# Two attention and gated-MLP layers on one core: new planner settings, a planned pause of GpSimd, and a last gate in two steps

## The chip, the core and the metric

The kernel runs on one core of a Trainium2 chip. A core has five engines that run side by side, each with its own instruction stream: TensorE (PE, matmuls; its weight loads are shown as PEld), VectorE (DVE), ScalarE (ACT), GpSimd (POOL) and SyncE (SP), which here issues the DMA transfers. They wait for each other on semaphores. Matmuls write to PSUM, which here is used as eight banks of 128 partitions by 512 fp32 values; the other tensors lie in SBUF. The metric is the device time of one execution in microseconds, lower being better, given as the median of several runs.

## The reference

A residual stream of 2048 tokens by 512 features passes through attention, a gated MLP, attention and a gated MLP; both attentions use the same weights, and so do both MLPs.

```python
x = x + attn(layernorm(x)); x = x + mlp(layernorm(x))      # and both once more

def attn(x):                       # 32 heads of 16, one shared key and value head
    q = (x @ wq) as 32 heads;  k = x @ wk;  v = x @ wv     # k, v: 2048 x 16
    p = softmax(q @ k.T / 4)                               # 32 x 2048 x 2048
    return heads(p @ v) @ wo

def mlp(x):                        # two halves of 896
    z = gelu(x @ w_in);  z1 = z[:, :896];  z2 = layernorm(z[:, 896:])
    g = w_sp @ z2 + b_sp[:, None]                          # mixes the 2048 tokens
    return (z1 * g) @ w_out
```

Inputs and output are bfloat16.

## The kernel before, in words

Nothing in the kernel's text fixes the order of instructions. The Python program builds a list of tasks with their dependencies, and a planner (`Sched`, and the `step_` functions of `Kernel`) walks through a model of time: whenever an engine is free in the model, its step function picks a task, and the pick is appended to that engine's stream. Only the order and the semaphore waits that the data need are emitted. A moment in which the planner left an engine idle on purpose is not in the program: on the chip an engine starts its next instruction as soon as its data and buffers are there. Every constant of the class (`SHARE`, `PV_EFF` and so on) is a setting of this planner.

**Attention.** The scores of one layer are 2048 blocks of 128 keys by 512 query columns. A score block is one matmul with a contraction of 32 rows, so four of them fit side by side in the array as row tiles; they are issued in packs of up to four (`issue_pack`, matmul at line 1227), each block to one PSUM bank. A block then goes one of two ways:

- to ScalarE (`pick_exp`, `do_exp`, line 1402), which takes exp of one block (128x512) or of two in adjacent banks (128x1024) and writes bfloat16 to slots of `Pb`, a pool of 32 slots of 128x512;
- to VectorE (`dve_block`), which approximates exp by three ramps in 16-bit integers whose bits are read as bfloat16. The first ramp reads PSUM (line 1316, task "A") and frees the bank. The second and third read the first ramp's slot (line 1335, tasks "S") and may run on GpSimd or on VectorE; two ramps whose sources lie in adjacent slots are joined into one instruction of 128x1024 (`commit_ramp`).

`SHARE`, `SHARE_HI` and `RAMP_SHARE` give the part of the blocks that goes to VectorE; the last is used while a layer's first two groups of query columns wait for their key tiles (`A.full` is not yet set).

P.V (`do_pv`, line 1457) multiplies each finished slot by V. Its output has 32 rows, so four matmuls run side by side as column tiles; a round is one matmul for each of up to four columns. `pv_depth` decides whether a round may start with fewer than four (`PV_EFF`, `PV_LEAST`) and how many rounds one task takes (`PV_MAX`). A change between score tiles, P.V tiles and full-size matmuls is a change of the array's shape, and the planner adds a cost for it in `commit`. When TensorE has been little used, `keep_warm` (line 1574) issues matmuls with zero weights.

**The rest.** Query columns are finished in eight chunks. After each, the sum is normalised, projected by `wo`, added to the residual `X` and normalised again (VectorE statistics, `L602`, `L603`; scaling on GpSimd or VectorE). Groups of chunks then enter the MLP: matmuls at lines 976 and 1022, gelu on ScalarE between two table loads. The token mixing (`spatial`) is done in five passes over source tiles; partial sums are kept in `gp` in fp16 (VectorE, line 1091). The last pass (`last_pass`) takes the last source tile: an identity matmul brings `gp` into PSUM (line 1114), the last product is added to it there (line 1116), VectorE multiplies by `z1` (line 1124), and the output projection (line 1138) and residual add (line 1142) follow. In layer 1 this overlaps with the opening of layer 2, in which each finished tile of `X` is normalised, transposed by DMA and turned into keys and values (lines 731 and 734); in layer 2 it is the tail of the kernel. SP's stream holds the loads, the transposing DMAs of tiles and of the mixing weights, and the 16 stores.

Of the kernel before, what the change touches and what calls it, by code (L numbers as in the profile page):

```python
# [92 lines left out]
class Sched:  # L93
# [69 lines left out]
    def commit(self, task, eng=None):  # L163
        t = self.t
        eng = eng or task.eng
        task.eng = eng
        if task.alts is not None:
            task.cost, task.fn = task.alts[eng]
        task.start = t
        if task.hook is not None:  # L170
            task.hook(task)
        cost = task.cost() if callable(task.cost) else task.cost
        occ, lat = cost
        if eng == "pe" and task.mode != self.pe_mode:
            occ += 100
            self.pe_mode = task.mode
        port = eng == "dve" and task.tag in PORT
        if port:
            occ += max(0.0, self.free["pool"] - t)
        end = t + occ  # L180
        self.free[eng] = end
        if port:
            self.free["pool"] = max(self.free["pool"], end)
        self.busy[eng] += occ
        task.done = end + lat
        waits = self._waits(eng, task)
        if eng == "sp":
            k = min(range(self.NDMA), key=lambda i: (self.dma_last[i].done if self.dma_last[i] else -1.0))
            prev = self.dma_last[k]
            if prev is not None:  # L190
                waits += self._wait_on(eng, prev)
            self.dma_n[k] += 16
            task.key, task.val = ("dma", k), self.dma_n[k]
            self.dma_last[k] = task
        else:
            self.cnt[eng] += 1
            task.key, task.val = eng, self.cnt[eng]
        s = dict(self.know[eng])
        if s.get(task.key, 0) < task.val:
            s[task.key] = task.val  # L200
        self.snap[(task.key, task.val)] = s
        self.prog[eng].append((waits, task.fn, task.key, task))
        self.log.append((eng, t, end, task.tag))
        if eng == "pe":
            self.pe_log.append((t, end))
        self.left -= 1
        for s_ in task.succ:
            s_.nopen -= 1
            if s_.nopen == 0:
                self._arm(s_)  # L210
        self.event(end)
        self.event(task.done)
        while self.after:
            self.after.pop(0)()
        return task
# [164 lines left out]
class Kernel:  # L380
# [4 lines left out]
    PV_FREE = 6  # L385
    KT_ACT = 16
    CREDIT = 2
    CAP_LINE = 8000
    RAMP_SHARE = 0.3
# [7 lines left out]
    SHARE = 0.3  # L397
    SHARE_HI = 0.32
# [3 lines left out]
    ACT_LOW = 1200  # L402
    POOL_MAX = 1400
    DVE_MAX = 1500
    DVE_HIGH = 2500
    PV_MIN = 3
    PV_MAX = 3
    PV_EFF = 0.7
    PV_LEAST = 4
    SLACK = 300  # L410
    SLACK_HI = 500
    MISC_T = 2000
    MISC_T2 = 1500
    MISC_T3 = 1000
    PE_LINE2 = 8000
    ACT_ONE = 3
# [688 lines left out]
    def last_pass(self, B, t, s0, n, sl, lds, zd, final, use):  # L1105

        tc, o = t // 4, (t % 4) * P
        hs = []
        for f0, f1 in ((0, 4), (4, NF)):
            def gf(e, b, lo, hi, f0=f0):  # L1110
                ins = None
                for f in range(lo, hi):
                    out = self.ps32[:, b, (f - f0) * P:(f - f0 + 1) * P]
                    e.matmul(out, self.ident16[:], self.gp[:, tc, f, o:o + P], start=True, stop=False)
                    for i in range(n):
                        ins = e.matmul(out, self.z2[:, (s0 + i) % 8, f * P:(f + 1) * P],
                                       self.wstr[:, sl[i // 4][1] + i % 4, o:o + P], start=False, stop=(i == n - 1))
                return ins
            m = f0 + 2

            def mk(lp, bank, f0=f0, f1=f1):
                def fn(e):
                    z = self.z1[:, tc, f0:f1, o:o + P]
                    return e.tensor_tensor(z, self.ps32[:, bank(), 0:(f1 - f0) * P].rearrange("p (f c) -> p f c", f=f1 - f0), z, ALU.mult)  # L1124
                return Task("dve", c_ps((f1 - f0) * P), fn, [lp] + B.z1g[tc], 0.9 + 0.08 * t, tag="gate")
            deps = [self.t_ident16] + [B.gpw[(tc, f)] for f in range(f0, f1)] + lds + zd
            made, outs = self.job(2 + 0.08 * t, [(lambda e, b, gf=gf, f0=f0, m=m: gf(e, b, f0, m), c_mm(2 * (n + 1), 128), deps),
                                                 (lambda e, b, gf=gf, m=m, f1=f1: gf(e, b, m, f1), c_mm((f1 - m) * (n + 1), 128), [])],
                                  [mk], "SPD", kind=B.layer, spare=1)
            hs += outs  # L1130
            use += made
            B.all += made
            self.gp_last.append(made[-1])
# [19 lines left out]
    def pack_ready(self):  # L1153
# [5 lines left out]
        if room < self.FILL_MIN or room < 4 and self.act_backlog() > self.ACT_LOW:  # L1159
# [9 lines left out]
        if not blks or len(blks) < room and len(blks) < 4 and A.nxt + len(blks) < len(A.blocks) and self.act_backlog() > self.ACT_LOW:  # L1169
# [20 lines left out]
    def issue_pack(self, A, blks, deps, bs):  # L1190
# [3 lines left out]
        x = self.RAMP_SHARE if not A.full else self.SHARE if self.pe_line() > self.PE_LINE else self.SHARE_HI  # L1194
# [11 lines left out]
        best = None  # L1206
        for act in itertools.combinations(sorted(bs, key=lambda b: b.i), len(aj)):
            runs = sum(1 for x, y in zip(act, act[1:]) if y.i != x.i + 1)
            key = (runs, sum(b.i for b in act))
# [44 lines left out]
    def slot_runs(self):  # L1254
        free = {b.i: b for b in self.pslots.avail()}
# [12 lines left out]
    def first_slot(self):  # L1268

        runs = self.slot_runs()  # L1270
        free = {b.i: b for r in runs for b in r}
# [22 lines left out]
    def dve_block(self, pk, u, kt, j, bank, n):  # L1294
# [10 lines left out]
        def h0(task):  # L1305
            b, paired = self.first_slot()
            slot(0, b, task, T)
            if not paired:
                self.open_slots.append(b.i)

            def go():
# [3 lines left out]
        lo0 = float(TERMS[0][0])  # L1315
        a = self.dve(c_ps(512), lambda e: e.tensor_scalar(self.Pi[:, sl[0].i, :], self.ps32[:, bank.i, :], EBIAS + lo0, lo0, op0=ALU.add,  # L1316
                                                          op1=ALU.max), [pk], 1.0, gate=lambda: self.slot_ok(n, 1), hook=h0, tag="A")
# [14 lines left out]

    def ramp_fn(self, v, src, dst, k):
        lo = float(TERMS[v][0])
        return lambda e: e.tensor_scalar(self.Pi[:, dst():dst() + k, :], self.Pi[:, src():src() + k, :], lo, 1.0, op0=ALU.add, op1=ALU.mult)  # L1335

    def commit_ramp(self, k, eng):

        s = self.s
        v, sl, n = k.ramp  # L1340
        for it in s.arm[eng]:
            p = it[2]
            if p.ramp is None or p.start is not None or p.ready > s.t or p.ramp[0] != v or abs(p.ramp[1][0].i - sl[0].i) != 1:
                continue
            m = max(n, p.ramp[2])
# [5 lines left out]
            two = sorted((k, p), key=lambda x: x.ramp[1][0].i)  # L1351
            i, o = two[0].ramp[1][0].i, run[0].i
            f = Task(eng, (c_pool if eng == "pool" else c_4x)(1024), self.ramp_fn(v, lambda: i, lambda: o, 2), k.deps + p.deps, tag="S")
# [7 lines left out]
            for x in two:  # L1361
                x.start, x.done, x.key, x.val = f.start, f.done, f.key, f.val
                s.left -= 1
            return
        s.commit(k, eng)

    def pick_exp(self):
        q = [x for x in self.act_q if x[0].done <= self.s.t][:self.ACT_MAX]
        av = sorted((b for b in self.pslots.items if not b.held and b.free <= self.s.t), key=lambda b: b.i)
# [149 lines left out]
    def pv_depth(self, pv, room):  # L1519
# [5 lines left out]
        if hurry:  # L1525
            most = max(most, 1)
        for r in range(most, 0, -1):
# [120 lines left out]
    def step_dve(self):  # L1648
        s = self.s
        k = s.pick("dve", lambda k: k.alts is None or "pool" not in k.alts)  # L1650
# [10 lines left out]

    def step_pool(self):
        k = self.s.pick("pool")
# [130 lines left out]
```

## Time and profile before

| | |
|---|---|
| median of 3 runs | 1654.17 us (1652.5 to 1657.26) |
| profiled execution | 1656.29 us |
| its span, first to last instruction | 1654.6 us |
| mean granted TensorE clock | 0.988 |
| exp on ScalarE (L1402) | 946 of 128x512, 948 of 128x1024 |
| first ramps on VectorE (L1316) | 1254 |
| second and third ramps (L1335) | GpSimd 976 of 128x512, 421 of 128x1024; VectorE 218 and 236 |
| score and P.V matmuls | 4096 and 6604 |

The span is what the trace covers. Busy time is the union of an engine's instructions; an instruction's own duration can overlap its neighbour's in the engine's pipeline, so durations can add up to more than the busy time. TensorE's ends are modelled, and a busy TensorE need not be at its peak. A row of the groups gives line, engine, operation, output and inputs with shapes, count, busy time, mean duration of one, and then the idle time of the engine just before such instructions with what ended it. A row of the waits gives who waited for whom, the total in us, the number of times and the longest.

### The profile page before, as it was taken

The numbers are of one execution on the slowest core, as the hardware profiler recorded it, in microseconds if no ns is written. First come the engines' busy times: TensorE is split into PE (matmuls) and PEld (weight loads), VectorE is DVE, ScalarE is ACT, GpSimd is POOL, SyncE is SP. The second block draws the span as 40 slices with busy tenths as digits, with TensorE's granted clock in tenths as the row PEclk, the third lists the DMA queues.
The fourth block names the chain that finished last, engine by engine and source line by source line (L and its number), as shares of the span: only waits on it lengthen the run. The fifth ranks groups of instructions, "written<-read, shape, count | busy, mean of one in ns | idle before, by whom it ended". The sixth has DMA issues, their size and how long they took to land.

```text
span 1654.6 us, 36692 instructions
## 1 busy us (share of the span) xinstructions
PE 1539.3 (93%) x13877; PEld 528.1 (32%) x14016; DVE 1405.0 (85%) x2556; ACT 1447.2 (87%) x2067; POOL 1182.1 (71%) x1616
## 2 busy tenths in 40 slices
PE   6999999999999999999988998999999999899998
PEld 3333233222322223233433332322223222222345
DVE  7899878898788887987978998788887998888877
ACT  5999999999899999995447999999998999899940
POOL 6878868778678767874456877777876778778730
PEclk8999999999999999999999999999999999999999
DMA  8000000100000110101110000011000101101021
GB/s 208 14 8 5 8 8 17 33 17 17 11 20 21 21 21 14 27 17 36 24 30 17 9 4 8 7 30 33 14 14 14 27 14 27 13 14 27 17 40 54
DMA packets 123996, 39.76 MB, mean 24 GB/s; under 512 B 116272, under 2 KB 123312, under 8 KB 123824
## 3 DMA queue, kind: packets, MB, share of 16 engines
q1 hardware_dynamic: 123824, 37.41, 10.7%
q8 instruction: 115, 1.88, 0.5%
q14 instruction: 57, 0.47, 0.1%
HBM read 6.98 MB, written 2.10 MB: 5 GB/s over the span
## 4 chain that ended last, share of the span: by engine, by line
PE 51%; ACT 30%; DVE 13%; issue 3%; POOL 2%; DMA 1%; SPq 0%; DVEq 0%; ACTq 0%; POOLq 0%
ACT Pb L1402 30%; PE ps_all L1457 16%; PE ps_all L1227 14%; PE ps_all L1083 7%; DVE Pb L1316 5%; PE ps_all L976 3%; PE ps_all L1022 3%; DVE Pb L1335 2%; PE ps_all L1138 2%; POOL Pb L1335 1%; PE ps_all L761 1%; DVE gp L1091 1%; PE ps_all L920 1%; PE ps_all L834 1%; DVE ln_st L602 1%
## 5 line engine op out<-in xcount | busy, mean ns | idle before, releaser
L1402 ACT ACTIVATE Pb<-ps_all 128x512 bf16<-128x512 f32 (+1 forms) x1894 | 1351.2, 884 | 78.7 <-PE ps_all L1227 66.9
L1335 POOL TENSOR_SCALAR Pb<-Pb 128x512 int16<-128x512 int16 (+1 forms) x1397 | 1064.1, 762 | 306.9 <-DVE Pb L1316 134.7
L1316 DVE TENSOR_SCALAR Pb<-ps_all 128x512 int16<-128x512 f32 x1254 | 830.0, 684 | 139.1 <-PE ps_all L1227 124.1
L1457 PE MATMUL ps_all<-Pb,V 128*32 128x512 bf16 x6604 | 628.4, 390 | 15.3 <-ACT Pb L1402 5.9
L1227 PE MATMUL ps_all<-Q,kT 32*128 32x512 bf16 x4096 | 572.6, 387 | 49.5 <-ACT Pb L1402 28.7
L1227 PEld LDWEIGHTS ps_all<-Q,kT 32*128 32x128 bf16 x4096 | 146.8, 91 | 543.6 <-ACT Pb L1402 309.6
L1457 PEld LDWEIGHTS ps_all<-Pb,V 128*32 128x32 bf16 x6604 | 150.2, 94 | 307.8 <-issue 125.9
L1335 DVE TENSOR_SCALAR Pb<-Pb 128x1024 int16<-128x1024 int16 (+1 forms) x454 | 205.0, 474 | 17.4 <-PE ps_all L1457 14.0
L1083 PE MATMUL ps_all<-wstr,z 128*128 128x512 bf16 x744 | 193.9, 380 | 18.0 <-issue 7.5
L1091 DVE TENSOR_TENSOR gp<-ps_all,gp 128x512 f16<-128x512 f32 x168 | 113.0, 687 | 26.4 <-PE ps_all L1083 24.6
L1083 PEld LDWEIGHTS ps_all<-wstr,z 128*128 128x128 bf16 x840 | 67.4, 98 | 102.7 <-issue 15.4
L1138 PE MATMUL ps_all<-w_out,z 128*128 128x512 bf16 x212 | 53.5, 380 | 3.1 <-DVE z L1124 0.8
L976 PE MATMUL ps_all<-w_in,xnT 128*128 128x448 bf16 x256 | 52.2, 360 | 2.6 <-DMA xnT<-xn 2.4
L1036 ACT ACTIVATE z<-ps_all 128x512 bf16<-128x512 f32 (+1 forms) x60 | 31.3, 566 | 23.6 <-PE ps_all L1022 23.6
L593 POOL TENSOR_SCALAR ln_rs<-ln_mv 128x1 f32<-128x1 f32 (+2 forms) x48 | 11.2, 237 | 56.3 <-DVE ln_mv L603 54.8
L1022 PE MATMUL ps_all<-xnT,w_in 128*128 128x512 bf16 (+2 forms) x274 | 50.2, 336 | 0.3
L818 DVE CAST oT<-ps_all 128x512 bf16<-128x512 f32 x64 | 43.7, 683 | 5.7 <-PE ps_all L1457 5.3
L989 DVE BATCH_NORM_STATS2 st<-z 128x6 f32<-128x448 bf16 x64 | 36.4, 607 | 12.3 <-ACT z L981 12.1
L1091 DVE TENSOR_TENSOR gp<-ps_all,bspc 128x512 f16<-128x512 f32 x56 | 38.4, 686 | 9.1 <-PE ps_all L1083 8.1
L602 DVE BATCH_NORM_STATS2 ln_st<-X 128x6 f32<-128x512 bf16 x64 | 43.2, 680 | 3.2 <-DMA X<-in_A_x_dram 3.0
L593 POOL TENSOR_SCALAR rs<-mv 128x4 f32<-128x4 f32 (+2 forms) x10 | 2.3, 234 | 55.9 <-DVE mv L991 55.9
L761 PE MATMUL ps_all<-z,wq 128*128 128x128 bf16 x512 | 40.7, 224 | 0.3 <-DVE Pb L1316 0.2
(67 smaller groups left out, 697.2 us busy)
## 6 DMA issues: line engine op xcount, KB each, us to landing
out_dram<-X SPq DMA_DIRECT2D x16, 128.0 KB, 1.7
w_in<-in_B_w_in_dram SPq DMA_DIRECT2D x1, 1792.0 KB, 12.0
X<-in_A_x_dram SPq DMA_DIRECT2D x3, 512.0 KB, 7.1
bspc<-in_B_b_sp_dram SPq DMA_DIRECT2D x8, 128.0 KB, 3.5
w_out<-in_B_w_out_dram SPq DMA_DIRECT2D x1, 896.0 KB, 12.7
wstr<-in_B_w_sp_dram SPq DMA_TRANSPOSE x40, 4.2
X<-in_A_x_dram SPq DMA_DIRECT2D x2, 256.0 KB, 3.6
wq<-in_A_wq_dram SPq DMA_DIRECT2D x1, 512.0 KB, 5.2
```

Source lines behind the costliest of these rows:

```text
L602: a = self.dve(c_ps(512), lambda e, t=t: e.bn_stats(st[:, t, :], X[:, t, :]), [dep], prio, tag="lnst")
L761: ins = e.matmul(self.ps32[:, b, g * P:(g + 1) * P], self.wq[:, kd, g * P:(g + 1) * P], self.xnT(t, kd), start=(kd == 0), stop=(kd == KD - 1))
L976: ins = e.matmul(self.ps32[:, b, 0:448], self.xnT2[:, buf, kd, o:o + P], self.w_in[:, kd, FH + h * 448:FH + (h + 1) * 448], start=(kd == 0 ...
L1022: ins = e.matmul(self.ps32[:, b, i * nq:(i + 1) * nq], self.w_in[:, kd, f * P:(f + 1) * P], self.xnT2[:, buf, kd, 0:nq], start=(kd == 0), ...
L1083: ins = e.matmul(self.ps32[:, b, :], self.z2[:, (s0 + i) % 8, f * P:(f + 1) * P], self.wstr[:, sl[i // 4][1] + i % 4, :], start=(i == 0), ...
L1091: return Task("dve", c_ps(512), lambda e: e.tensor_tensor(self.gp[:, tc, f, :], self.ps32[:, bank(), :], src, ALU.add), dps, 1.05, tag="gp")
L1138: ins = e.matmul(self.ps32[:, b, :], self.z1[:, tc, f, o:o + P], self.w_out[:, f, :], start=(f == 0), stop=(f == NF - 1))
L1227: ins = e.matmul(self.ps32[:, jb[i].i, :], self.kT[32 * j:32 * j + 32, u.half, kt * P:(kt + 1) * P], q, tile_position=(32 * j, 0), start=T ...
L1316: a = self.dve(c_ps(512), lambda e: e.tensor_scalar(self.Pi[:, sl[0].i, :], self.ps32[:, bank.i, :], EBIAS + lo0, lo0, op0=ALU.add, op1=AL ...
L1335: return lambda e: e.tensor_scalar(self.Pi[:, dst():dst() + k, :], self.Pi[:, src():src() + k, :], lo, 1.0, op0=ALU.add, op1=ALU.mult)
L1402: return e.activation(self.Pb[:, s0:s0 + n, :], self.ps32[:, b0:b0 + n, :], ACTF.Exp, scale=ESCALE)
L1457: ins = e.matmul(self.ps32[32 * j:32 * j + 32, u.bank.i, :], self.V[:, var, kt, :], self.Pb[:, sl.i, :], tile_position=(0, 32 * j), start= ...
```

## The change

The change has four parts.

1. *Settings.* More blocks for VectorE in the full part of a layer (`SHARE` 0.30 to 0.32, `SHARE_HI` 0.32 to 0.34), none in the opening of layer 2 (`RAMP_SHARE1` 0), where score packs are issued only four at a time (`FILL_R` 4, `ACT_LOW_R` 0). P.V rounds are planned only when full (`PV_EFF` 0.7 to 0.97), a change to P.V's shape needs six or more matmuls (`PV_LEAST`), one task takes at most two rounds. `ACT_ONE` 3 to 9 lets ScalarE join two blocks more often or less, by what is queued; `DVE_HIGH` and the `MISC_T` settings move too, and the planner's cost for a change of shape goes from 100 to 110 ns.
2. *Slots kept for pairs.* Where a first ramp has taken a slot, a free neighbour is kept (`kept`) for the next one, so that the later ramps of both can be joined, as long as eight other slots are free. Banks for blocks of VectorE are chosen adjacent where possible.
3. *Pairs on VectorE, and the pause.* When GpSimd's planned backlog is over 4000 ns and GpSimd is free in the plan, VectorE first looks for two joinable ramps (`ramp_pair`). When VectorE will be free within 200 ns, GpSimd takes nothing in the plan (`HOLD`).
4. *The last gate of layer 2* (`NOID`). The identity matmuls are left out; VectorE adds the PSUM product to `gp` in place, and GpSimd multiplies `z1` by `gp`. Layer 1 is left as it was.

```diff
-            occ += 100
+            occ += 110
-    PV_FREE = 6
+    PV_FREE = 8
+    KEEP = 8
+    POOL_TOP = 4000
+    HOLD = 200
+    A_ADJ = 1
-    SHARE = 0.3
-    SHARE_HI = 0.32
+    SHARE = 0.32
+    SHARE_HI = 0.34
+    FILL_R = 4
+    NOID = (False, True)
+    ACT_LOW_R = 0
+    RAMP_SHARE1 = 0.0
-    DVE_HIGH = 2500
+    DVE_HIGH = 1800
-    PV_MAX = 3
-    PV_EFF = 0.7
-    PV_LEAST = 4
+    PV_MAX = 2
+    PV_EFF = 0.97
+    PV_LEAST = 6
-    ACT_ONE = 3
+    ACT_ONE = 9
...
     def last_pass(self, B, t, s0, n, sl, lds, zd, final, use):
-                    e.matmul(out, self.ident16[:], self.gp[:, tc, f, o:o + P], start=True, stop=False)
+                    if not noid:
+                        e.matmul(out, self.ident16[:], self.gp[:, tc, f, o:o + P], start=True, stop=False)
...
+            if noid:
+                def pf(e, f0=f0, f1=f1):
+                    z = self.z1[:, tc, f0:f1, o:o + P]
+                    return e.tensor_tensor(z, self.gp[:, tc, f0:f1, o:o + P], z, ALU.mult)
+                outs = [self.pool((240 + self.PTT * (f1 - f0) * P, 60), pf, outs + B.z1g[tc], 0.9 + 0.08 * t, tag="gatep")]
...
+    def kept(self):
+        free = {b.i for b in self.pslots.avail()}
+        r = set()
+        for i in self.open_slots:
+            for k in (i + 1, i - 1):
+                if k in free and k not in r:
+                    r.add(k)
+                    break
+        return r if len(free) - len(r) >= self.KEEP else set()
...
     def step_dve(self):
+        if s.free["pool"] <= s.t + self.PORT_WAIT and self.backlog("pool") > self.POOL_TOP:
+            k = self.ramp_pair("dve")
+        if k is None:
+            k = s.pick("dve", lambda k: k.alts is None or "pool" not in k.alts)
...
     def step_pool(self):
-        k = self.s.pick("pool")
+        if s.t < s.free["dve"] <= s.t + self.HOLD and self.backlog("pool") > self.POOL_TOP:
+            return False
```

## The prediction

> **What bounds the kernel now.** I read the busy totals first, then the busy time by stage, then the waits of ScalarE, then one microsecond-scale stretch of TensorE, then the prices by shape. The totals:
>
> ```profile
> PE 1539.3 (93%) x13877; PEld 528.1 (32%) x14016; DVE 1405.0 (85%) x2556; ACT 1447.2 (87%) x2067; POOL 1182.1 (71%) x1616
> ```
>
> Four engines are nearly full, so the average decides nothing. I cut the span at ScalarE's table loads, which separate ten stages of exp from the gelu batches, and asked for busy time in each. Columns: window, length, then PE, PEld, DVE, ACT, POOL busy (instructions), clock, DMA share, GB/s.
>
> ```profile
> 0.00:229.40 229.40, 204.40 (x2073) 72.87 (x2077) 196.02 (x385) 206.68 (x300) 177.94 (x256) 0.97 0.19 45
> 241.50:419.40 177.90, 166.55 (x1520) 49.51 (x1529) 158.15 (x278) 175.30 (x237) 141.66 (x190) 1.00 0.11 22
> 785.70:1048.30 262.60, 240.68 (x2395) 92.75 (x2407) 229.42 (x436) 205.34 (x299) 180.13 (x254) 1.00 0.08 16
> 1448.60:1563.20 114.60, 109.64 (x988) 33.98 (x996) 101.25 (x175) 112.73 (x159) 92.04 (x121) 1.00 0.10 21
> 1607.70:1654.60 46.90, 42.49 (x357) 25.68 (x361) 34.43 (x59) 1.45 (x2) 0.30 (x1) 1.00 0.17 54
> ```
>
> ScalarE idles 2.6 us of 177.9 and 1.9 of 114.6; over the eight exp stages other than the first of each layer it idles 20 of 977 us. There ScalarE sets the time. Not in the stage that opens layer 2 (57.3 idle of 262.6) and in the tail, where it has no work. Its waits agree:
>
> ```profile
> ACT Pb L1402 <- PE ps_all L1227: 66.9, 73, 10.9
> ACT Pb L1402 <- PE ps_all L1457: 7.1, 13, 1.4
> ```
>
> The first (waiting for scores) lies mostly in the layer openings: 40.0 us of it between 786 and 880. The second is ScalarE waiting until a P.V round frees a Pb slot; it is small now. TensorE:
>
> ```profile
> 314.24 0.40 PE L1457 MATMUL ps_all<-Pb,V 128*32 128x512 bf16 x4
> 314.57 0.39 PE L1227 MATMUL ps_all<-Q,kT 32*128 32x512 bf16 x3
> 314.90 0.83 PE L1457 MATMUL ps_all<-Pb,V 128*32 128x512 bf16 x10
> 315.66 0.39 PE L1227 MATMUL ps_all<-Q,kT 32*128 32x512 bf16 x3
> ```
>
> From start to start, one round takes 0.33 us and three rounds (x10) 0.76: 0.215 us a round, however many of its four column tiles are used, and 0.11 us for each change between score, P.V and full shape.
>
> Prices (busy, mean ns of one):
>
> ```profile
> L1402 ACT ACTIVATE Pb<-ps_all 128x1024 bf16<-128x1024 f32 x948 | 953.2, 1098 | 51.7 <-PE ps_all L1227 45.7 <-PE ps_all L1457 3.8 <-DVE Pb L1335 0.6
> L1316 DVE TENSOR_SCALAR Pb<-ps_all 128x512 int16<-128x512 f32 x1254 | 830.0, 684 | 139.1 <-PE ps_all L1227 124.1 <-PE ps_all L1457 4.0
> L1335 POOL TENSOR_SCALAR Pb<-Pb 128x512 int16<-128x512 int16 x976 | 615.1, 630 | 225.8 <-DVE Pb L1316 111.5 <-PE ps_all L1457 40.5 <-DVE Pb L1335 10.0
> L1335 POOL TENSOR_SCALAR Pb<-Pb 128x1024 int16<-128x1024 int16 x421 | 448.9, 1066 | 81.1 <-DVE Pb L1316 23.3 <-PE ps_all L1457 23.0 <-DVE Pb L1335 7.8
> L1335 DVE TENSOR_SCALAR Pb<-Pb 128x1024 int16<-128x1024 int16 x236 | 130.9, 570 | 9.1 <-PE ps_all L1457 6.3 <-POOL Pb L1335 0.4
> L1335 DVE TENSOR_SCALAR Pb<-Pb 128x512 int16<-128x512 int16 x218 | 76.8, 370 | 8.3 <-PE ps_all L1457 7.7
> ```
>
> Exps overlap their neighbours, so these means are too high for a sum: in the instruction records, start to start without idle, a 512 exp takes 0.486 us on average and a 1024 one 0.916.
>
> **What the Trainium skill says.** "Perfetto Trace Analysis", Identifying the Most-Contended Engine: matmul busy time is a poor measure of TensorE. It agrees: 1,985 P.V and some 1,355 score rounds at 0.215, 2,679 changes at 0.11 and some 430 us of full-shape matmuls make 1,440 us, not 1,539. "TensorEngine Tiling (Array Packing)", Key Properties: changing the tiling mode drains TensorE; the 0.11 us above is that. "GPSIMD Engine Reference", Specifications: GpSimd's SBUF interfaces are shared with VectorE, which contends when VectorE runs in a two-port mode. The records show it: of 236 paired ramps on VectorE 93 began with GpSimd idle and took 0.364 us, 143 began inside a GpSimd operation and took 0.615 (up to 1.25; the wait ends with that operation). Singles: 0.209 against 0.441.
>
> **The change, part by part**, from the order in which both programs stand.
>
> *ScalarE.* 512 exps 946 to 956, 1024 exps 948 to 923: 10 x 0.486 - 25 x 0.916 = -18.1 us. By stage it is more useful: first stage of layer 1 (163 and 132 become 173 and 121) -5.2; the other four of layer 1 -11.0; first stage of layer 2 (167 and 126 become 128 and 156) +8.5, since its opening gives VectorE no block any more; the other four of layer 2 -10.4. Where ScalarE is full these are the path: -5.2 - 11.0 - 10.4 = -26.6. The +8.5 falls where it idles.
>
> *Opening of layer 2.* From the first residual add at 792 to the last key tile at 885 the pace is VectorE's and TensorE's (8.5 to 9.5 us busy in each 10). Ahead of the last key tile stand 92 score blocks instead of 120, 88 P.V matmuls instead of 182 and 54 shape changes instead of 112. TensorE saves 58 x 0.11 + about 28 rounds of P.V and 9 of scores x 0.215 = 14 us; VectorE about 36 first ramps x 0.605 (start to start) = 22. Both cover the same time: I take 18. ScalarE does 92 x 0.47 = 43 us there instead of about 84 x 0.47 = 39. Its idle time falls by 18 + 4 = 22, the stage by 22 - 8.5 = 13.5. On SP's queue one weight slab moves ahead of ten of the opening's tile transposes; it waits for layer 1's last gate to free its buffer, and keys behind it wait too. So the ends are 0 (the opening hangs on that, or on LayerNorm chains) and 22. The other slabs move by a transpose or three, among transfers that no engine waits long for.
>
> *TensorE elsewhere.* P.V rounds 1,985 to 1,737 (full ones 1,117 to 1,623), changes 2,679 to 2,265, identity matmuls 224 to 112, 120 more warming matmuls (30 rounds): -248 x 0.215 - 414 x 0.11 - 112 x 0.055 + 6 = -99 us. Outside the opening and the tail it is hidden behind ScalarE; I count nothing. It buys banks sooner for ScalarE, which has only 20 us left to regain.
>
> *VectorE.* First ramps +40 x 0.662 (830.0/1254) = +26; paired ramps +135 x 0.555 = +75; single ones -107 x 0.352 = -38: +64 us. It is hidden by 181 us of VectorE idle in the ten exp stages; with stages 40 us shorter about 77 remain. That thin a cover leaks: a late VectorE frees score banks late. I allow 10.5 us, about 1% of the saturated stretches, between 0 and 30. The pause is in the planner only: nothing holds GpSimd on the chip, so a pair may meet an operation just begun.
>
> *GpSimd.* -393 x 0.630 + 155 x 1.066 = -82 us; it idles already.
>
> *Last gate, layer 2, all in the tail.* TensorE loses 112 identity matmuls at 0.055: -6.2. VectorE's 32 adds cost what its multiplies did (0.679 and 0.547). New: 32 GpSimd multiplies with two inputs, which no row shows. Lower end, GpSimd's one-input price: 0.63 and about 0.5, 1.1 us a tile, hidden behind TensorE's 1.9 (7 x 0.055 + 7 x 0.215). Upper end, an estimate from "GPSIMD Engine Reference", Elementwise, side-by-side cycle accounting (2.6 cycles an element at 1.2 GHz) with 0.19 us of start: 1.30 + 1.02 = 2.3 us a tile, 37 for 16, and the tail is then GpSimd's: first gate at 1613, products to about 1651, then the last projection, add and store, as now. The tail gains 6 or nothing: -2. The 16 stores keep their place behind the adds.
>
> **Sum.** -26.6 - 13.5 - 2 + 10.5 = -31.6, against the profiled execution (1656.3, span 1654.6, 1.7 around it): 1624.7. It stands 2.1 above the median of the runs, so 1622 as a median.
>
> **Rivals.**
> 1. *The port takes it.* If every ramp on VectorE meets a busy GpSimd, ramps cost 371 x 0.615 + 111 x 0.441 = 277 us against 186 now; with +26 that is 118 more on 1,288 busy in 1,469 us of exp stages. At the most that VectorE can be full, say 96.5%, they need 1,457: 12 saved, with the tail 14: 1640. For it: GpSimd was busy at 143 of 236. Against: GpSimd has 82 us less to do.
> 2. *More than the sum:* pairs find GpSimd idle (0.364), VectorE's load falls, no allowance, opening -22, tail -6: -55, 1600.
> 3. *Slower: slots.* Full rounds hold Pb slots longer, and slots are kept for pairs. 365 exps now wait for a P.V matmul in the program, 306 before. Today 13 such waits cost 7.1 us, 0.55 each. The 42 us of gain before the allowance are gone when 77 of the 365 cost that; at 102 the time is 1668. Against: the share of exps that wait so hardly rises.
> 4. *Nothing:* a gain in ScalarE work that comes back as idle of equal size: 1654.
>
> **How the numbers follow.** Sum as worked 0.50 (own range 1608 to 1635), rival 1 0.17, rival 2 0.18, rival 3 0.10, rival 4 0.05. A measurement tells about 0.3%, 5 us. Faster 0.85, same 0.05, slower 0.10. The range 1597 to 1650 leaves out the low end of rival 2, rival 3 and most of rival 4.
>
> **What would show it.** Right: exp groups near 956 and 923 with ScalarE idle still under 5 us in the middle stages; about 250 us for the opening stage of layer 2; ScalarE's wait for P.V under 20 us; VectorE about 1,470 busy. Wrong: pairs near 0.8 us and VectorE at 97% of a stage; ScalarE waiting 50 us on P.V; a GpSimd multiply over 1.4 us with TensorE idle in the tail.

## The result and the profile after

The changed kernel takes 1643.24 us (median of 4 runs, 1641.84 to 1645.47), the kernel before 1655.72 beside it (4 runs, 1652.5 to 1657.65). The ratio is 0.9928 with a 95% interval of 0.9906 to 0.9949: 12 us faster. Forecast were 1622 and a range of 1597 to 1650. The direction and the range held; of the gain of 32 us only 12 came.

The totals of the changed kernel, from its page:

```profile
PE 1480.0 (90%) x13974; PEld 498.6 (30%) x14104; DVE 1452.0 (89%) x2624; ACT 1441.8 (88%) x2052; POOL 1139.3 (69%) x1410
```

TensorE has become lighter by 59 us of busy time and GpSimd by 43; VectorE is busy for 47 us more. The span fell from 1654.6 to 1640.1, and ScalarE is busy for 5 us less, not for 18. The busy time in the stages between ScalarE's table loads, for the same five stages as before (window, length, PE, PEld, DVE, ACT, POOL, clock, DMA share, GB/s):

```profile
0.00:229.60 229.60, 194.85 (x2092) 68.41 (x2096) 208.59 (x405) 204.06 (x299) 166.42 (x237) 0.98 0.21 45
243.00:417.60 174.60, 161.66 (x1526) 46.79 (x1532) 164.69 (x293) 170.04 (x241) 134.87 (x159) 0.98 0.11 22
788.90:1037.50 248.60, 218.77 (x2370) 86.36 (x2380) 208.94 (x402) 214.24 (x289) 128.48 (x172) 0.99 0.08 15
1434.20:1554.10 119.90, 110.41 (x1046) 33.84 (x1055) 113.85 (x198) 114.88 (x155) 94.03 (x112) 1.00 0.12 20
1598.90:1640.10 41.20, 36.22 (x241) 18.44 (x243) 32.52 (x57) 1.52 (x3) 32.20 (x33) 1.00 0.20 61
```

The gain is in the third row, the stage that opens layer 2 (262.6 to 248.6), and in the last, the tail (46.9 to 41.2). In the second row ScalarE now idles 4.6 us and VectorE 9.9; before it was 2.6 and 19.8. Summed over the eight exp stages other than the first of each layer (the middle stages from here on), VectorE went from 88.3% to 93.4% busy and ScalarE's idle time from 20.0 to 39.5 us. The waits, ScalarE's first, then TensorE's waits for VectorE to free a bank before scores:

```profile
ACT Pb L1460 <- PE ps_all L1252: 61.8, 120, 5.8
ACT Pb L1460 <- PE ps_all L1515: 7.9, 23, 0.8
PEld ps_all L1252 <- DVE Pb L1374: 135.9, 298, 1.4
PE ps_all L1252 <- DVE Pb L1374: 33.1, 87, 1.1
```

ScalarE waits for a score pack 120 times instead of 73. The wait for P.V (second line) stayed small. The last two lines, score packs waiting for VectorE, were in the kernel before:

```profile
PEld ps_all L1227 <- DVE Pb L1316: 84.1, 204, 1.1
PE ps_all L1227 <- DVE Pb L1316: 6.9, 19, 0.8
```

One stretch of TensorE in the changed kernel:

```profile
300.48 0.39 PE L1252 MATMUL ps_all<-Q,kT 32*128 32x512 bf16 x3
300.80 0.62 PE L1515 MATMUL ps_all<-Pb,V 128*32 128x512 bf16 x8
301.35 0.39 PE L1252 MATMUL ps_all<-Q,kT 32*128 32x512 bf16 x3
```

Two full rounds (x8) take 0.55 us start to start with their change of shape, as 2 x 0.215 + 0.11 says. The prices by shape (busy, mean ns of one):

```profile
L1460 ACT ACTIVATE Pb<-ps_all 128x1024 bf16<-128x1024 f32 x923 | 923.8, 1069 | 54.6 <-PE ps_all L1252 44.3 <-PE ps_all L1515 4.3 <-DVE Pb L1379 1.2
L1374 DVE TENSOR_SCALAR Pb<-ps_all 128x512 int16<-128x512 f32 x1294 | 842.6, 680 | 86.7 <-PE ps_all L1252 78.5 <-PE ps_all L1515 1.5
L1379 POOL TENSOR_SCALAR Pb<-Pb 128x512 int16<-128x512 int16 x583 | 371.4, 637 | 185.0 <-DVE Pb L1374 91.8 <-PE ps_all L1515 52.3 <-DVE Pb L1379 4.1
L1379 POOL TENSOR_SCALAR Pb<-Pb 128x1024 int16<-128x1024 int16 x576 | 615.8, 1069 | 155.0 <-DVE Pb L1374 86.4 <-PE ps_all L1515 26.2 <-DVE Pb L1379 8.4
L1379 DVE TENSOR_SCALAR Pb<-Pb 128x1024 int16<-128x1024 int16 x371 | 222.1, 618 | 5.9 <-PE ps_all L1515 4.6
L1379 DVE TENSOR_SCALAR Pb<-Pb 128x512 int16<-128x512 int16 x111 | 40.9, 375 | 3.3 <-PE ps_all L1515 3.3
```

A paired ramp on VectorE became dearer, 618 ns on average instead of 570. The instruction records say why. Of 371 pairs 161 began with GpSimd idle and took 0.347 us; 210 began inside a GpSimd operation and took 0.704 us. Of those 210, 119 met an operation that had started less than 0.3 us earlier; before it was 48 of 143. Not every pair that began inside an operation waited for it: 43 of the 210 ended before it, after 0.33 us, and 167 ended after it (17 and 126 before). The plan has no such meetings. In `commit`, in both kernels, GpSimd counts as busy until a second or third ramp of VectorE has ended, and in the changed kernel it also idles for the last 200 ns before VectorE comes free, so that VectorE's pair goes first. Nothing in the program of either kernel makes GpSimd wait for the pair. In the stretch below it waits only for the first ramp that VectorE has just finished (the brackets give its idle time and what ended it), so the same moment frees VectorE for two pairs and releases GpSimd, which starts before the second of them. The timeline of VectorE, then of GpSimd:

```profile
556.22 1.60 DVE L1379 TENSOR_SCALAR Pb<-Pb 128x1024 int16<-128x1024 int16 x2
557.74 1.27 DVE L1374 TENSOR_SCALAR Pb<-ps_all 128x512 int16<-128x512 f32 x2
558.94 1.59 DVE L1379 TENSOR_SCALAR Pb<-Pb 128x1024 int16<-128x1024 int16 x2
```

```profile
556.39 1.15 POOL L1379 TENSOR_SCALAR Pb<-Pb 128x1024 int16<-128x1024 int16 x1 [1.72 <-DVE Pb L1374]
559.10 1.15 POOL L1379 TENSOR_SCALAR Pb<-Pb 128x1024 int16<-128x1024 int16 x1 [1.55 <-DVE Pb L1374]
```

Twice GpSimd, idle for over 1.5 us, starts 0.16 to 0.17 us after the first of two pairs on VectorE has begun, and 0.25 us before that pair ends. In the records VectorE comes free at 556.64; the second pair, then inside GpSimd's operation, ends at 557.82. Two pairs take 1.6 us instead of the 0.75 that they need alone (e_wait, below).

### The profile page after: what moved, and what is told of

Same layout as the page of the kernel before. It is cut to its first block, busy times and chain, and to the rows that moved or that the text cites. A ratio compares the mean times of both kernels' runs of the same rounds, so it can differ in the third digit from the quotient of the medians.

```text
span 1640.1 us, 36572 instructions
## 1 busy us (share of the span) xinstructions
PE 1480.0 (90%) x13974; PEld 498.6 (30%) x14104; DVE 1452.0 (89%) x2624; ACT 1441.8 (88%) x2052; POOL 1139.3 (69%) x1410
## 4 chain that ended last, share of the span: by engine, by line
PE 38%; DVE 31%; ACT 22%; issue 4%; POOL 3%; DMA 1%; POOLq 0%; SPq 0%; DVEq 0%; ACTq 0%
ACT Pb L1460 21%; DVE Pb L1374 16%; PE ps_all L1252 11%; PE ps_all L1515 11%; DVE Pb L1379 8%; PE ps_all L1095 6%; PE ps_all L988 3%; PE ps_all L1034 3%; DVE gp L1103 2%; POOL z L1150 2%; PE ps_all L1160 1%; DVE ln_st L614 1%; PE ps_all L773 1%; DVE oT L830 1%; DMA z<-xn 1%
## 5 line engine op out<-in xcount | busy, mean ns | idle before, releaser
L1379 POOL TENSOR_SCALAR Pb<-Pb 128x512 int16<-128x512 int16 (+1 forms) x1159 | 987.3, 852 | 340.0 <-DVE Pb L1374 178.1
L1374 DVE TENSOR_SCALAR Pb<-ps_all 128x512 int16<-128x512 f32 x1294 | 842.6, 680 | 86.7 <-PE ps_all L1252 78.5
L1252 PE MATMUL ps_all<-Q,kT 32*128 32x512 bf16 x4096 | 583.6, 388 | 92.8 <-ACT Pb L1460 35.5
L1515 PE MATMUL ps_all<-Pb,V 128*32 128x512 bf16 x6684 | 526.6, 390 | 15.4 <-DVE Pb L1379 4.4
L1252 PEld LDWEIGHTS ps_all<-Q,kT 32*128 32x128 bf16 x4096 | 153.2, 91 | 620.0 <-ACT Pb L1460 361.4
L1379 DVE TENSOR_SCALAR Pb<-Pb 128x1024 int16<-128x1024 int16 (+1 forms) x482 | 260.1, 562 | 9.2 <-PE ps_all L1515 7.9
L1095 PE MATMUL ps_all<-wstr,z 128*128 128x512 bf16 x748 | 194.9, 380 | 19.1 <-issue 5.9
L1515 PEld LDWEIGHTS ps_all<-Pb,V 128*32 128x32 bf16 x6684 | 119.0, 95 | 235.2 <-issue 114.2
L830 DVE CAST oT<-ps_all 128x512 bf16<-128x512 f32 x64 | 43.4, 680 | 19.4 <-PE ps_all L1515 19.4
```

The source lines that it names most:

```text
L830: ev = Task("dve", c_ps(512), lambda e, u=u, k=k: e.tensor_copy(self.oT[:, k, :], self.ps32[:, u.bank.i, :]), [self.oT_use[k]], 0.2, tag=" ...
L1095: ins = e.matmul(self.ps32[:, b, :], self.z2[:, (s0 + i) % 8, f * P:(f + 1) * P], self.wstr[:, sl[i // 4][1] + i % 4, :], start=(i == 0), ...
L1252: ins = e.matmul(self.ps32[:, jb[i].i, :], self.kT[32 * j:32 * j + 32, u.half, kt * P:(kt + 1) * P], q, tile_position=(32 * j, 0), start=T ...
L1515: ins = e.matmul(self.ps32[32 * j:32 * j + 32, u.bank.i, :], self.V[:, var, kt, :], self.Pb[:, sl.i, :], tile_position=(0, 32 * j), start= ...
```

## The experiments

Theory V: the middle stages lost their gain because VectorE is too full, above all through pairs that meet a GpSimd operation just begun. Rival P: the rule of full P.V rounds holds back scores and slots. Smaller questions are the tail and the opening of layer 2. Each ratio is to executions of the kernel before on the same chip.

| run | edit | median us | ratio (95%) | middle stages, ScalarE idle in them | opening of layer 2 | tail |
|---|---|---|---|---|---|---|
| before | | 1655.7 | | 976.7, 20.0 | 262.6 | 46.9 |
| changed | | 1643.2 | 0.9928 (0.9906 to 0.9949) | 984.3, 39.5 | 248.6 | 41.1 |
| e_wait | changed, pause real | 1600.5 | 0.9672 (0.9642 to 0.9701) | 956.2, 19.1 | 243.0 | 41.1 |
| e_half | changed, half of the waits | 1613.6 | 0.9739 (0.9697 to 0.9781) | 964.8, 25.8 | 244.1 | 41.1 |
| f_wait | before, the waits of e_wait | 1644.6 | 0.9941 (0.9918 to 0.9963) | 966.4, 12.6 | 258.5 | 47.3 |
| e_nopair | no pairs first, no pause | 1652.8 | 0.9987 (0.9967 to 1.0007) | 963.2, 43.4 | 273.1 | 41.1 |
| e_share | fewer blocks on VectorE | 1648.9 | 0.9961 (0.9946 to 0.9976) | 980.5, 19.6 | 253.9 | 42.9 |
| e_wait30 | e_wait, fewer blocks | 1629.4 | 0.9852 (0.9818 to 0.9886) | 965.7, 8.2 | 248.7 | 42.9 |
| e_wait34 | e_wait, more blocks | 1605.2 | 0.9686 (0.9650 to 0.9721) | 952.6, 33.9 | 245.8 | 41.7 |
| e_pv | P.V rule undone | 1651.8 | 0.9974 (0.9962 to 0.9986) | 943.3, 25.1 | 281.1 | 52.6 |
| e_waitpv | e_wait, P.V rule undone | 1621.7 | 0.9799 (0.9766 to 0.9832) | 926.3, 13.6 | 267.3 | 52.6 |
| f_pv | before with the P.V rule | 1646.5 | 0.9944 (0.9916 to 0.9972) | 981.3, 15.1 | 257.4 | 44.3 |
| e_open | opening as before | 1659.6 | 1.0019 (0.9999 to 1.0039) | 991.1, 47.2 | 266.2 | 44.2 |
| e_noid | last gate as before | 1648.5 | 0.9953 (0.9933 to 0.9972) | 979.8, 35.3 | 251.4 | 45.7 |

The stage lengths are those of one profiled execution each; that of e_pv took 10.5 us more than the median of its kernel and that of e_open 12 us more, that of e_nopair 8 us less, so the stages of these rows are somewhat long or short. Where an edit makes the planner place blocks elsewhere, work moves between the middle stages and the openings, so single columns of such rows are not to be compared; of e_wait, e_half and e_noid the order of the attention work is that of the changed kernel.

**The pause made real (e_wait).** The edit in `commit` (`self.pair` is None at the start) makes the first GpSimd instruction that the plan has behind a second or third ramp of VectorE wait for that ramp. So both things that only the plan knew hold on the chip: the pause, and the older rule that GpSimd does not start before the ramp has ended.

```diff
+        if eng == "pool" and self.pair is not None:
+            task.extra = task.extra + [self.pair]
+            self.pair = None
+        if eng == "dve" and task.tag == "S":
+            self.pair = task
         waits = self._waits(eng, task)
```

> Edit: the changed kernel with the same instructions in the same order, but the GpSimd instruction that the planner puts behind a second or third ramp of VectorE now waits for that ramp, so that the pause exists on the chip. Theory V (the middle stages lost their gain because VectorE is too full, above all by paired ramps that begin inside a GpSimd operation, 210 of 371 at 0.70 us): pairs fall to 0.35 to 0.50 us, VectorE's busy time by 30 to 70 us, ScalarE's idle time in the eight middle stages from 40 to under 30 us, the time to 1622 to 1636. Rival P (the rule of full P.V rounds holds back scores and slots): the price of a pair falls but the time stays within 4 us of 1643. Rival G (GpSimd's results become late by the waits, and P.V waits for them): 1648 to 1665.

Measured: 1600.5 us, faster than theory V asked for, and 43 us below the changed kernel. Only waits were added. The paired ramps of e_wait, its waits of ScalarE, and two middle stages:

```profile
L1385 DVE TENSOR_SCALAR Pb<-Pb 128x1024 int16<-128x1024 int16 x371 | 154.5, 436 | 6.8 <-PE ps_all L1521 5.0
```

```profile
ACT Pb L1466 <- PE ps_all L1258: 46.2, 77, 5.3
ACT Pb L1466 <- PE ps_all L1521: 2.2, 7, 0.6
```

```profile
238.50:409.50 171.00, 164.14 (x1547) 47.21 (x1537) 158.64 (x293) 169.02 (x240) 130.71 (x159) 1.00 0.11 23
421.40:593.40 172.00, 162.98 (x1557) 47.02 (x1556) 159.75 (x288) 169.04 (x247) 131.31 (x162) 1.00 0.11 20
```

The same 371 pairs cost 436 ns instead of 618. In the records 92 of them still meet GpSimd, but only 5 an operation begun within 0.3 us, against 119. VectorE is busy for 1391 us instead of 1452. ScalarE waits for scores 77 times, as rarely as before the change, and the middle stages take 956.2 us, 28 less. The timeline of VectorE, then of GpSimd, in a like stretch of e_wait:

```profile
542.78 0.75 DVE L1385 TENSOR_SCALAR Pb<-Pb 128x1024 int16<-128x1024 int16 x2
543.45 1.28 DVE L1380 TENSOR_SCALAR Pb<-ps_all 128x512 int16<-128x512 f32 x2
544.65 0.75 DVE L1385 TENSOR_SCALAR Pb<-Pb 128x1024 int16<-128x1024 int16 x2
```

```profile
543.62 1.04 POOL L1385 TENSOR_SCALAR Pb<-Pb 128x1024 int16<-128x1024 int16 x1 [1.17 <-DVE Pb L1385]
545.49 1.74 POOL L1385 TENSOR_SCALAR Pb<-Pb 128x1024 int16<-128x1024 int16 x2 [0.82 <-DVE Pb L1385]
```

GpSimd starts once VectorE's two pairs are done, beside the first ramps, which read PSUM; two pairs take 0.75 us.

Theory V had looked at the middle stages alone. They give 28 of the 43 us: ScalarE idles 20 us less there and is busy for 8 us less. The opening of layer 2 gives 5.6, the first stage 3.7 and the gelu batches 4.0. A higher clock is not the reason: the two profiled executions had a mean granted TensorE clock of 0.987 and 0.988 and differ by 41 us.

**Half of the waits (e_half).** The same edit, with

```diff
-            self.pair = task
+            self.nth += 1
+            self.pair = task if self.nth % 2 else None
```

> Edit: as e_wait, but the wait stands behind every second second-or-third ramp of VectorE only; order and counts are those of the changed kernel. Theory V (the time follows the price of the ramps): pairs cost between the 0.55 us of the changed kernel and the 0.37 us of e_wait, and the time lies about half way between 1643 and 1601, 1612 to 1632. If a single place in the plan made the difference, it would be at either end.

Measured: 1613.6 us, with

```profile
L1387 DVE TENSOR_SCALAR Pb<-Pb 128x1024 int16<-128x1024 int16 x371 | 174.2, 489 | 6.9 <-PE ps_all L1523 5.4
```

The pairs lie between the two ends, and so does the time. In the records the second and third ramps on VectorE, pairs and single ones, take 236.7 us in the changed kernel, 185.7 here and 164.1 in e_wait: half of the waits saves 51 of 73 us, 70%, and the time falls by 30 of 43 us, 69%. The gain follows the price of the ramps.

**The same waits in the kernel before (f_wait).** The diff of e_wait, on the kernel before. That kernel has no planned pause; what becomes real is the older rule alone.

> Edit: the kernel before, with the same instructions in the same order, but the GpSimd instruction behind a second or third ramp of VectorE waits for that ramp. Theory V (what the meetings of VectorE's ramps with GpSimd cost counts where VectorE is full): here VectorE is 88% busy in the middle stages and ScalarE idles only 20 us there, so the ramps get cheaper by 30 to 50 us and the time falls by at most 5 to 18 us, 1636 to 1650. Rival W (the wait is worth the same in any plan): 42 us less, 1608 to 1616.

Measured: 1644.6, 11 us below the kernel before, as theory V had it. The records give VectorE's ramps 154 us instead of 186, so they became cheaper by 32 us, of which the kernel kept a third; ScalarE had little idle time to give back. The same waits are worth 43 us in the changed kernel. So with the waits in both kernels the change is worth 44 us, and not 12.

**No pairs first, no pause (e_nopair).**

```diff
-    POOL_TOP = 4000
+    POOL_TOP = 1000000000
```

> Edit: POOL_TOP from 4000 to one billion, so neither the search for pairs on VectorE nor the planned pause happens; 300 pairs and 57 single ramps are left on VectorE instead of 371 and 111, GpSimd has 789 pairs and 361 singles. Theory V: VectorE is relieved of about 50 us, the middle stages shorten by 10 to 20 us, 1623 to 1634. Rival P: within 4 us of 1643. Rival G (GpSimd is then behind and P.V waits for it): slower than 1646.

Measured: 1652.8. Theory V missed by 19 us, although VectorE was relieved about as it said (1452 to 1408 us busy, 90% in the middle stages). The middle stages are 21 us shorter, as it had said too, but the opening of layer 2 is 24 us longer. Of the 300 pairs 178 still begin inside a GpSimd operation and take 0.655 us. The waits of ScalarE:

```profile
ACT Pb L1460 <- PE ps_all L1252: 48.4, 90, 5.5
ACT Pb L1460 <- PE ps_all L1515: 25.2, 47, 1.5
```

GpSimd now has the ramps (1139 to 1215 us), and ScalarE waits 25.2 us for P.V to free slots instead of 7.9. So taking pairs to VectorE seems to buy something, namely slots in time, and theory V is a part of the account, not all of it: VectorE and GpSimd both hold ScalarE up when they get more to do. This edit undoes the search for pairs and the pause together; the pause alone (`HOLD`) was not undone in any run.

**Fewer blocks on VectorE (e_share), and the same with the pause real (e_wait30).**

```diff
-    RAMP_SHARE = 0.32
-    SHARE = 0.32
-    SHARE_HI = 0.34
+    RAMP_SHARE = 0.30
+    SHARE = 0.30
+    SHARE_HI = 0.32
```

> Edit: SHARE, SHARE_HI and RAMP_SHARE back to 0.30, 0.32 and 0.30: 73 blocks go back from VectorE to ScalarE. ScalarE gains about 35 us of work, VectorE loses 44 us of first ramps and about 40 of later ones. Theory V: ScalarE's idle time in the middle stages falls by 15 to 25 us against about 30 us of added work there, so 1645 to 1660 and ScalarE over 97% busy there. Rival P: the idle time of ScalarE stays near 40 us, so 1668 to 1680.

> Edit: e_wait with SHARE, SHARE_HI and RAMP_SHARE back to 0.30, 0.32 and 0.30; the same instructions in the same order as e_share, with the waits. Theory V (with the pause real, ScalarE sets the middle stages again, so a block moved to VectorE pays there): 73 blocks more on ScalarE are about 35 us of exp, some of it in the openings, so 1622 to 1636, against 1601 of e_wait; without the pause the same move cost only 6 us (e_share 1649 against 1643). Rival: the share does not matter with the pause either, 1598 to 1610.

Measured: 1648.9 and 1629.4, both as theory V had them. In e_share the idle time of ScalarE went back to 19.6 us: the 73 blocks moved to VectorE had been paid for with waits. By the medians, moving them gains 6 us without the pause and 29 us with it. The 6 us are not clear: the two intervals overlap, and e_share ran at a lower granted clock (0.970 to 0.981 against 0.981 to 0.987); its three executions at 0.980 and 0.981 took 1640 to 1647 us, about as long as the changed kernel. The 29 us are beyond the intervals, and ScalarE is busy for 32 us more in e_wait30 than in e_wait.

**More blocks on VectorE with the pause (e_wait34).** The same three settings at 0.34, 0.34 and 0.36.

> Edit: e_wait with SHARE 0.34, SHARE_HI 0.36 and RAMP_SHARE 0.34. VectorE gets 76 first ramps more (46 us) and some 25 us of later ones, ScalarE 29 us less by its prices. Theory V: in e_wait VectorE is 92% busy in the middle stages and takes about half of this before it is full as in the changed kernel, so ScalarE's idle time grows again: 1592 to 1612. If ScalarE alone bounded e_wait: 1570 to 1580.

Measured: 1605.2. ScalarE is busy for 19 us less than in e_wait (1410.9 against 1430.2), VectorE is 95% busy in the middle stages, and ScalarE's idle time there grows from 19.1 to 33.9 us. So a fuller VectorE costs waits with the pause real too; but it is fuller here than in the changed kernel (93%), which is 38 us slower. The intervals of e_wait and e_wait34 overlap, so the two can't be told apart; both are over 3% below the kernel before.

**The P.V rule (e_pv, e_waitpv, f_pv).**

```diff
-    PV_FREE = 8
-    PV_MAX = 2
-    PV_EFF = 0.97
-    PV_LEAST = 6
+    PV_FREE = 6
+    PV_MAX = 3
+    PV_EFF = 0.7
+    PV_LEAST = 4
```

f_pv is the reverse edit on the kernel before.

> Edit: PV_EFF, PV_LEAST, PV_MAX and PV_FREE back to 0.7, 4, 3 and 6, all else as in the changed kernel. Theory V: TensorE was hidden, VectorE is as full as before, the time is between 1640 and 1655. Rival P: ScalarE's idle time in the middle stages falls to about 20 us and the time to 1620 to 1632.

> Edit: e_wait with PV_EFF 0.7, PV_LEAST 4, PV_MAX 3 and PV_FREE 6; the same instructions in the same order as e_pv, with the waits. By the prediction's step TensorE is hidden in the middle stages: the time stays within 12 us of 1601. Rival (full P.V rounds are a part of the gain once VectorE is relieved): 1620 to 1640.

> Edit: the kernel before with PV_EFF 0.97, PV_LEAST 6, PV_MAX 2 and PV_FREE 8. By the prediction's step TensorE is hidden in the middle stages, so nothing is gained there and at most the opening of layer 2 shortens: 1644 to 1656. Rival P turned round (fewer rounds and shape changes are worth time by themselves): 1620 to 1640. The planner then also leaves more single exps (1096 instead of 946), which costs ScalarE about 35 us of work: if that shows, 1665 to 1690.

Measured: 1651.8, 1621.7 and 1646.5. Rival P falls: without the rule the changed kernel is slower, not faster. f_pv stays where "TensorE is hidden" puts it: its middle stages are 4.6 us longer than those of the kernel before, its opening of layer 2 is 5.2 us shorter. The additional single exps cost ScalarE 2 us of busy time and not 35, since there are 78 fewer of two blocks. But e_waitpv met the rival of its own expectation: the rule is worth 21 us beside e_wait, more than the 12 that its expectation allowed. It is not the exp stages that pay: the ten together take 1427.1 us in e_waitpv and 1425.1 in e_wait. The tail grows from 41.1 to 52.6 us and the gelu batches from 132.5 to 141.7, together 21 us. In the tail of e_waitpv stand 72 mixing matmuls of 512 columns (line 1095 of the changed kernel), against 20 in e_wait; at 0.215 us the difference is 11 us. Other rows agree: f_pv has 14 of them and a tail of 44.3 us, the kernel before 25 and 46.9; the changed kernel has 20 and 41.1, e_share 29 and 42.9, e_open 35 and 44.2. So without the rule more of TensorE's full-size work is left for the tail, where nothing covers it. Why the planner leaves it there, and what makes the gelu batches longer, was not followed up. Against the kernel before, the changed one spares only 1 us there (20 for 25); what the rule does is keep the other settings from pushing work into the tail.

**The opening of layer 2 (e_open) and the last gate (e_noid).**

```diff
-    FILL_R = 4
-    ACT_LOW_R = 0
-    RAMP_SHARE1 = 0.0
+    FILL_R = 2
+    ACT_LOW_R = 1400
+    RAMP_SHARE1 = 0.32
```

> Edit: FILL_R 2, ACT_LOW_R 1400 and RAMP_SHARE1 0.32 in the changed kernel, so the opening of layer 2 is planned as the full part is. By the prediction's step the stage that opens layer 2 grows from 249 us back towards 263: 1652 to 1662. Rival: the opening was made shorter by the full P.V rounds alone, and the time stays within 4 us of 1643.

```diff
-    NOID = (False, True)
+    NOID = (False, False)
```

> Edit: NOID (False, False): the last gate of layer 2 again with identity matmuls and a multiply on VectorE; all other counts are as in the changed kernel. If the two-step gate is what shortened the tail from 46.9 to 41.2 us, the tail is 46 to 47 us and the time 1647 to 1651. Rival: the tail got shorter by another order of work in it, and the time stays within 2 us of 1643.

Measured: 1659.6 and 1648.5, each time within its expectation. The opening stage grows from 248.6 to 266.2 us, and ScalarE idles 63.3 us in it instead of 34.4, so its settings hold the gain. The tail grows from 41.1 to 45.7 us, with as many mixing matmuls in it: the two-step gate is worth 4.6 us there.

## Why the prediction was right or wrong

**ScalarE's work, -26.6 (first stage of layer 1 and the middle stages).** The premise held once VectorE was not late: 32 us more work for ScalarE made e_wait30 29 us slower than e_wait. In the changed kernel the work did not fall by as much: its busy time in the middle stages went from 956.7 to 944.8 us, -12 where the sum had -21. In the records of these stages 80 exps began after idle time in the kernel before, in the changed kernel 160. A 128x512 exp after idle time takes 597 ns, one behind another adds 490 from end to end (128x1024: 1023 and 917), so the 80 more cost 9 us of busy time. With the pause real there are 93 of them, and ScalarE is busy for 937.1 us, 19.6 less than in the kernel before.

**VectorE, "I allow 10.5 us, about 1% of the saturated stretches, between 0 and 30".** This step failed. Measured, the first stage and the middle stages together became 7.8 us longer where the sum had 26.6 less: 34 us lost, above even the upper end of the allowance. Of these, 22 are more idle time of ScalarE (65 us in these stages, 43 before) and 12 are work that it did not save. The load itself was about right (+64 forecast, +47 measured), but idle time of VectorE was no cover at 93% busy: score packs waited longer for its banks, and ScalarE for the scores. e_wait gives back 32 of the 34 us by changing only when GpSimd starts. The kernel before has such meetings of the two engines as well, and the same waits give it 9 us in these stages (f_wait). So about 22 of the 34 us are what the meetings cost the change more than they cost the kernel before. With the waits in both kernels these stages gain 15 us, not 26.6; where the other 12 are lost stays open.

**"The pause is in the planner only: nothing holds GpSimd on the chip, so a pair may meet an operation just begun."** This was seen, of the pause and not of the rule that GpSimd stays idle in the plan until such a ramp ends, and then priced at the average of the kernel before (0.555 us a pair; the page now gives 222.1/371 = 0.599). But the new order brings such meetings about: 119 of 371 pairs began inside an operation younger than 0.3 us, against 48 of 236, and 58 of the 119 operations had been released by a first ramp of VectorE, as in the stretch above, against 17 of the 48. In e_nopair, without pairs first and without the pause, it is 71 of 300, with 13 so released. Which of the two settings does it was not tried. The argument against rival 1, that GpSimd has 82 us less to do, missed this. And "the wait ends with that operation" is not quite what the records of the kernel before show: 126 of 143 pairs ended after it, as a rule by 0.28 us, and 17 did not wait.

**Rival 1 (the port takes it, 1640)** named the place, and the time within 3 us, but that time is partly luck. It asked for 118 us more of VectorE's work in the exp stages and for a VectorE that is 96.5% full; measured were 49 us more and 93.4% in the middle stages. Of the pairs 57% meet GpSimd, not all, and each of these costs 0.704 us, not 0.615.

**Opening of layer 2, -13.5:** measured -14.0, and ScalarE's idle time there fell from 57.3 to 34.4 us where the step had 22 less. e_open shows that the gain goes when these settings are undone.

**Tail, -2:** measured -5.8, of which e_noid gives 4.6 to the gate; five fewer mixing matmuls at 0.215 us are the rest. GpSimd's multiplies take, start to start, 1.11 us for four row blocks and 0.87 for three, 1.98 a tile. The rows:

```profile
L1150 POOL TENSOR_TENSOR z<-gp,z 128x512 bf16<-128x512 f16 x16 | 18.7, 1170 | 4.4 <-DVE gp L1139 4.4
L1150 POOL TENSOR_TENSOR z<-gp,z 128x384 bf16<-128x384 f16 x16 | 14.9, 932 | 0.0
```

The upper end, 2.3 us a tile as estimated from the Trainium skill, "GPSIMD Engine Reference", Elementwise, side-by-side cycle accounting, was too dear by 16%. From the first to the last of the 32 multiplies GpSimd has no gap, and in the tail it is busy for 32.2 of 41.2 us; that it sets the tail is argued from this and was not tried.

**TensorE elsewhere, nothing:** against the kernel before this held in the middle (f_pv). It was incomplete as a rule: without the full rounds the tail and the gelu batches of the changed plan are 21 us longer (e_waitpv).

**Rival 3 (slots)** did not happen: the wait for P.V is 7.9 us after 7.1. **Rivals 2 and 4** did not happen either. What rival 2 described is what e_wait did: pairs at 0.367 us on average where it had 0.364, and 1600.5 us where it had 1600.

**The signs.** Those named for "right" held but for one: the exp counts, 248.6 us for the opening, 7.9 us of waiting for P.V and 1452 us of VectorE came about as said, and ScalarE's idle time in the middle stages did not (39.5 us in sum, over 5 us in five of the eight stages, before in one). None of those named for "wrong" came. So the totals did not give the failure away; the idle time of the engine that sets the time did.

## What to carry to other kernels

A pause that a planner leaves between instructions, or a rule of its model that two engines take turns, does not exist on the chip unless a semaphore makes it; an order that depends on it can produce the very collision that it avoids. When work moves onto an engine to relieve the one that bounds, look at how full the receiver becomes in the stage where it matters, and at what its instructions cost beside the neighbour's there, not on average. An added wait can be a gain: here 43 us. The same wait was worth 11 us to the kernel before, so before a whole gain is laid to what a change made worse, the cure has to be tried on the old kernel too.

## What the runs showed of the hardware

- A paired VectorE ramp in int16 on SBUF takes 0.347 us on average in the changed kernel when GpSimd is idle. One that begins inside a GpSimd operation mostly waits for its end and then takes about 0.28 us: of 210 such pairs in the changed kernel 167 ended after the operation, all at least 0.28 us after it. In the record that begins when VectorE comes free at 556.64 us it lasted 1.18 us.
- The other 43 did not wait; they took 0.33 us, and half of them had begun within 0.12 us of the start of the operation. Where it was a 128x1024 ramp, GpSimd paid: 1.25 to 1.36 us instead of the 1.043 that the ramp takes alone.
- 312 waits of GpSimd for VectorE's ramps, 189.8 us in all in e_wait, brought more than they cost: ScalarE waits 2.2 us for P.V there, where the changed kernel has 7.9, so GpSimd's results did not come too late.
- GpSimd's multiply of two inputs (fp16 and bfloat16) takes (1.11 - 0.87)/128 = 1.9 ns per element of a partition.
